# Early attention rows of a fused attention, FFN and DFT kernel: a unit's turn issued behind the next unit's scores, operands in three fixed tiles, and the second block's rows turned by TensorE

## The chip, the cores and the metric

The kernel runs on one core of a Trainium2 chip. The metric is the time of one execution on the device in microseconds (us). Five engines take part: TensorE (PE in the rows, with its weight loads as PEld), VectorE (DVE), ScalarE (ACT), GpSimd (POOL) and SyncE (SP), which here only issues transfers (DMAs). Each engine works its own instructions off in the order in which they stand, and semaphores hold it where it needs another engine's result.

## What is computed

```python
def reference(**kwargs):
    ...
    attn_out = _attn_ref(**attn_kwargs)      # 4 batches, 8 heads, 576 rows, head size 64
    x = np.ascontiguousarray(attn_out.transpose(0, 2, 1, 3)).reshape(B, S, H * D)
    x = _moe_ref(x=x, **moe_kwargs)          # LayerNorm, 512 -> 2048, relu, 2048 -> 512, + x
    return _moe2_ref(x=x, **moe2_kwargs)     # x + Re(FFT2(x)), LayerNorm, second FFN, + u
```

Attention is causal by blocks of 64 rows: a row sees the keys up to the end of its own block. The softmax is `exp(scores - max) / (sum + 1e-9)`. Weights, inputs and outputs are float32.

## The kernel before, in words

The 576 rows of a batch are cut into blocks of 256 rows: E(b), the first 256 rows of batch b, F(b), another 256, and L, the 64 rows left of each of the four batches together. The program has three long parts: the early rows E0 to E3 with the first FFN of E0 and E1 and the decoding of the first FFN's weights (the first 150 us), the attention of all other rows with the first FFN of the rest, then the DFT and the second FFN. Float32 products are made of float16 pairs (a high and a low part, three products each), and the weights, which arrive as wide words, are decoded by ACT (L214, a sign copy), DVE (L215), ACT again (a sum of squares, L236), POOL (a sum over partitions), DVE (scales), ACT (L328, the high part) and DVE (L336, the low part). The first FFN's first weight has four quarters, which the built program calls wq110 to wq113; the quarter c serves the steps mp = 2c and 2c + 1 of the FFN's first product.

**Early rows.** A batch's early rows are worked off in four units, one for each pair of heads (`e_items`, L1029). A unit loads its operands into a tile `raw` (`e_raw`, L866: a query part and two key parts, each with the other half of its partitions set to zero by POOL, L872), forms its scores on TensorE (`e_s`, L932; lines L937 and L905), takes the maximum on DVE (L951, L952) and the exponential on ACT (L955). For E0 and E1 (the tuple `ET`) the unit's exponentials are then turned, keys to partitions, by TensorE itself against a unit matrix (`e_turn`, L961; line L966), copied by ACT to a tile `PT` (L971) and multiplied with the values in float32 (`e_pv`, L983; line L990); for E2 and E3 they are split into two float16 parts (L909 on ACT, L910 on DVE) and turned by a transposing DMA (L916), and the product with the values is L885. `e_x` (L1010) divides by the sum and writes the block's rows `X`. The scores' PSUM tiles have two buffers, so a unit's scores wait until the unit before the last has left them: for E0 and E1 that is the copy L971, since the turn writes into the scores' own tile.

**LayerNorm of a block.** `ln` (L520) computes mean and scale on DVE, `ln_hi` (L554) normalizes into `xn` (L561). For E0 the normalized rows are turned by TensorE (`ln_turn`, L571: eight matmuls of line L575 into two PSUM tiles `xt`, copied by ACT at L580, the rest formed by DVE at L581). For every other block ACT and DVE make the float16 parts (`xs`, L568 and L588) and two transposing DMAs on SP's queue turn them (L589). The result `xnT` is what the block's first product waits for.

**First product.** `gemm1` (L604) is one step of 24 matmuls (L621) into one PSUM tile; ACT and DVE empty it (L630, L631). The tiles of `xt`, of `gemm1` and of the second product come from one pool (`g_tile`, L112, tag `g`), which has two buffers in this part of the program and gives them in the order in which the tiles are asked for:

```python
        ps = g_tile([128, 4, 128], "xt")      # L573, ln_turn
        ps = g_tile([128, 2, 256], "g1")      # L615, gemm1
```

**What sets the order.** `merge` (L1273) interleaves several streams of steps by weights and start times, and a scheduler then orders each engine's instructions by what is ready and by priority (`prio`). Within the streams here, `LN` holds the LayerNorm steps of E0 and E1 at a high priority, `AE` the early rows, `WA` and `WB1` the weights. `in_order` (L1265) makes a function's instructions stand behind the last TensorE instruction issued so far.

Of the kernel before, what the change touches and what calls it, by code (L numbers as in the profile page):

```python
# [8 lines left out]
F32 = mybir.dt.float32  # L9
# [11 lines left out]
NPAIR = H // 2  # L21
# [5 lines left out]
G2P = 1  # L27
ST = 2
RVE = 1
RAWE = 2  # L30
AP = 20
DW = (3, 5)
DW2 = (("G1", 1, ("F", 3), 7),) * 2 + (("F", 1, ("F", 3), 0), ("F", 1, ("F", 3), 1))
# [19 lines left out]
GSB = 2  # L53
LNQ = 200
X0B = 2
G1E = 1
LNA = 2
ESP = 20
# [38 lines left out]
def fused_kernel(ctx: ExitStack, tc: tile.TileContext, io: dict):  # L97
# [455 lines left out]

    def ln_hi(ffn, c, t):  # L554
        mv, y = lnst[ffn, c]
        own = (ffn, c) == (1, ("E", 0))
        if own:
            xn = a_tile([128, DM], F32, "xn0", "xn0")
        else:
            xn = fpool.tile([128, DM], F32, tag="xn", bufs=1, name="xn")  # L560
        nc.vector.tensor_scalar(  # L561
            out=xn, in0=X[c][:, t, :], scalar1=mv[:, t, 0:1], scalar2=y[:, t:t + 1],
            op0=ALU.subtract, op1=ALU.mult,
        )
        if own:
            return ln_turn(ffn, c, t, xn)
        xs = fpool.tile([128, 2, DM], F16, tag="xs", bufs=1, name="xs")
        nc.scalar.activation(out=xs[:, 0, :], in_=xn, func=AF.Copy)  # L568
        lnst[ffn, c, t] = (xn, xs)
# [11 lines left out]
        nc.vector.tensor_tensor(out=to[:, 1], in0=ps, in1=to[:, 0], op=ALU.subtract)  # L581

    def ln_lo(ffn, c, t):
        if (ffn, c) == (1, ("E", 0)):
            return
        xn, xs = lnst.pop((ffn, c, t))
        eng = nc.gpsimd if (ffn, t) in LNP else nc.vector
        eng.tensor_tensor(out=xs[:, 1, :], in0=xn, in1=xs[:, 0, :], op=ALU.subtract)  # L588
        nc.sync.dma_start_transpose(  # L589
            out=xnT[ffn, c].rearrange("p a k t -> p (a k) t")[:, :, t * 128:(t + 1) * 128],  # L590
            in_=xs.rearrange("p a f -> p (a f)"),
        )
# [222 lines left out]
    def a_tile(shape, dt, tag, name):  # L815
        return ap_["p"].tile(shape, dt, tag=tag, bufs=ap_["b"][tag], name=name)
# [48 lines left out]

    def e_raw(b, p):  # L866

        r = a_tile([128, 3, 256], F32, "raw", f"raw{b}{p}")
        nc.sync.dma_start(out=r[:, 0], in_=io["qt"][b, p][:, S:S + 256])
        for h in range(2):  # L870
            hs = slice(64 * h, 64 * h + 64)
            nc.gpsimd.memset(r[64 - 64 * h:128 - 64 * h, 1 + h], 0.0)  # L872
            nc.sync.dma_start(out=r[hs, 1 + h], in_=io["kt"][b, p][hs, 0:256])
        A["raw", b, p] = r

# [151 lines left out]
        )  # L1027

    def e_items(b):  # L1029
        def head():  # L1030
            e_raw(b, 0)
            e_load(b)

        def front(p):
            if p + 1 < NPAIR:
                e_raw(b, p + 1)
            e_s(b, p)
            e_exp(b, p)
            e_norm_p(b, p)

        def back(p):
            e_pv(b, p)
            e_x(b, p)

        out = [(0.0, head, (), None), (3.0, lambda: front(0), (), None)]
        if b not in ET:
            out.append((1.0, lambda: e_v(b), (), None))
        for p in range(1, NPAIR):
            out.append((3.0, lambda p=p: (front(p), back(p - EL) if p >= EL else None), (), None))
        for p in range(NPAIR - EL, NPAIR):  # L1050
            out.append((1.0, lambda p=p: back(p), (), ("X1", ("E", b)) if p == NPAIR - 1 else None))
        return out
# [455 lines left out]
    if True:  # L1508
# [28 lines left out]
            dft_setup(dctx)  # L1537

        ap_["first"] = True
        a_open(dict(stage=ST, rv=RVE, raw=RAWE, vh=2, vl=2, e=E1B[0], P=E1B[1], PT=E1B[2], xnT0=1, xn0=X0B, unit=1))  # L1540
        A["unit"] = a_tile([128, 128], F32, "unit", "unit")
        nc.gpsimd.dma_start(out=A["unit"], in_=io["c_unit"])
        w_signs(ap_["p"], WN[0], NZ[0])
        AE = [e_items(b) for b in range(B)]
# [208 lines left out]
```

## Time and profile before

| what | us |
|---|---|
| three runs, median (lowest to highest) | 994.23 (993.83 to 995.99) |
| the profiled execution | 991.83 |
| its span on the core | 990.1 |
| PE busy in the span | 925.9 (94%) |
| DVE, ACT, POOL busy in the span | 706.0, 541.5, 85.6 |
| PE waits of 0 to 60, 60 to 120 and 120 to 200 us that the profile names, summed | 14.7, 8.8, 5.8 |

The profiled execution took 1.73 us more than its span, and 2.40 us less than the median of the runs. How to read the views: a timeline's row gives the start, the length, the engine, the line and what it wrote and read, then how many instructions it merges, and in brackets how long the engine had been idle just before and what ended that. A busy PE is not PE at its peak, since matmuls are pipelined.

### The profile page before, as it was taken

The numbers are of one execution on the slowest core, as the hardware profiler recorded it, in microseconds if no ns is written. First come the engines' busy times: TensorE is split into PE (matmuls) and PEld (weight loads), VectorE is DVE, ScalarE is ACT, GpSimd is POOL, SyncE is SP. The second block draws the span as 40 slices with busy tenths as digits, with TensorE's granted clock in tenths as the row PEclk, the third lists the DMA queues.
The fourth block names the chain that finished last, engine by engine and source line by source line (L and its number), as shares of the span: only waits on it lengthen the run. The fifth ranks groups of instructions, "written<-read, shape, count | busy, mean of one in ns | idle before, by whom it ended". The sixth has DMA issues, their size and how long they took to land.

```text
span 990.1 us, 19844 instructions
## 1 busy us (share of the span) xinstructions
PE 925.9 (94%) x7794; PEld 701.4 (71%) x7794; DVE 706.0 (71%) x1753; ACT 541.5 (55%) x963; POOL 85.6 (9%) x216
## 2 busy tenths in 40 slices
PE   6797898998989898997999889999999999999998
PEld 5686744674664674856585666858588888888887
DVE  2888898777877786656597888679477675765754
ACT  4888757776776686427556544326153252342431
POOL 2101110002011020040011120100000000000000
PEclk9999999999999999999999999999999999999999
DMA  6759654677667585577318657002110101101100
GB/s 218 225 201 238 161 120 117 129 136 160 126 138 150 131 148 99 97 171 299 107 38 243 212 182 231 16 12 74 34 23 23 42 13 33 23 24 42 23 23 22
DMA packets 161566, 111.50 MB, mean 113 GB/s; under 512 B 136509, under 2 KB 143686, under 8 KB 159424
## 3 DMA queue, kind: packets, MB, share of 16 engines
q1 hardware_dynamic: 159120, 105.92, 41.9%
q0 software_dynamic: 2352, 4.32, 1.9%
q8 instruction: 61, 1.00, 0.4%
q14 instruction: 33, 0.27, 0.1%
HBM read 64.19 MB, written 11.01 MB: 76 GB/s over the span
## 4 chain that ended last, share of the span: by engine, by line
PE 47%; DVE 5%; DMA 4%; ACT 3%; issue 1%; POOL 0%; SPq 0%; ACTq 0%; POOLq 0%; DVEq 0%
PE g L692 15%; PE s L742 13%; PE g L621 9%; PE g L673 4%; PE g L646 4%; DMA wr<-in_w 3%; PE ya L1413 1%; ACT junk L236 1%; DVE ws L215 1%; DVE wq L336 1%; ACT sign L214 1%; DMA xnT2('F', 0)_8352<-xs 1%; DMA d<-ws 1%; PE pq L1447 0%; PE pv L885 0%
## 5 line engine op out<-in xcount | busy, mean ns | idle before, releaser
L621 PEld LDWEIGHTS <-wq 128*128 128x128 f16 x2112 | 206.3, 99 | 48.0 <-issue 7.8
L646 PE MATMUL g<-wq,hT 128*128 128x512 f16 x768 | 186.4, 381 | 1.3 <-ACT hT L630 1.2
L692 PEld LDWEIGHTS <-wq 128*128 128x128 f16 x1344 | 131.5, 98 | 15.4
L646 PEld LDWEIGHTS <-hT 128*128 128x128 f16 x768 | 74.1, 98 | 83.8 <-issue 2.3
L709 ACT ACTIVATE hr<-g,tk 128x256 f32<-128x256 f32 x112 | 47.0, 471 | 142.8 <-PE g L692 142.8
L742 PEld LDWEIGHTS <-hs 128*128 128x128 f16 x1176 | 115.1, 98 | 13.3
L885 PE MATMUL pv<-vh,PT 128*128 128x65 f16 (+1 forms) x704 | 97.2, 200 | 8.7 <-DMA PT<-P 4.6
L885 PEld LDWEIGHTS <-PT 128*128 128x128 f16 x1056 | 76.0, 98 | 34.2 <-issue 11.7
L717 DVE TENSOR_TENSOR hr<-hr 128x128 f32<-128x128 f32 x224 | 65.5, 292 | 48.3 <-ACT hr L709 40.4
L1134 PE MATMUL st<-k,qz 128*128 128x512 f16 (+2 forms) x288 | 80.3, 332 | 15.1 <-ACT e L1156 13.4
L1156 ACT ACTIVATE e<-st,aq,acf 128x384 f32<-128x384 f32 (+2 forms) x80 | 56.8, 741 | 52.7 <-DVE aq L1151 48.6
L910 DVE SCALAR_TENSOR_TENSOR P<-e,P 128x768 f16<-128x768 f32 (+2 forms) x56 | 54.4, 974 | 33.7 <-ACT P L909 33.4
L742 PE MATMUL s<-tT,hs 128*128 128x256 f16 x672 | 75.6, 273 | 0.0
L631 DVE SCALAR_TENSOR_TENSOR hT<-g,hT 128x512 f16<-128x512 f32 x88 | 59.8, 683 | 17.2 <-ACT hT L630 17.1
L630 ACT ACTIVATE hT<-g 128x512 f16<-128x512 f32 x88 | 51.3, 587 | 30.6 <-PE g L621 30.4
L673 PE MATMUL g<-wq,hT 128*128 128x512 f16 x288 | 64.0, 379 | 0.0
L724 DVE TENSOR_TENSOR hs<-hr,hs 128x896 f16<-128x896 f32 x56 | 60.8, 1085 | 0.5
L214 ACT ACTIVATE sign<-wr 128x512 f16<-128x512 bf16 (+1 forms) x48 | 46.4, 970 | 23.0 <-DMA wr<-in_w 22.9
L885 PE MATMUL pv<-vl,PT 128*128 128x64 f16 (+1 forms) x352 | 58.2, 199 | 0.0
L742 PE MATMUL s<-tB,hs 128*128 128x256 f16 x504 | 57.3, 273 | 0.0
L215 DVE SCALAR_TENSOR_TENSOR ws<-wr,sign 128x512 int32<-128x512 int32 (+1 forms) x48 | 41.3, 866 | 20.3 <-ACT sign L214 18.5
L723 ACT ACTIVATE hs<-hr 128x896 f16<-128x896 f32 x56 | 53.2, 949 | 1.6 <-DVE hr L717 1.6
(427 smaller groups left out, 1610.2 us busy)
## 6 DMA issues: line engine op xcount, KB each, us to landing
wr<-in_w SPq DMA_DIRECT2D x16, 1023.5 KB, 5.6
wr<-in_w SPq DMA_DIRECT2D x32, 511.8 KB, 5.1
rawv<-in_vt SPq DMA_DIRECT2D x16, 320.0 KB, 3.6
rawqk<-in_kt SPq DMA_DIRECT2D x16, 288.0 KB, 2.8
d<-ws SPq DMA_DIRECT2D x4, 1024.0 KB, 5.0
ws<-d SPq DMA_DIRECT2D x4, 1024.0 KB, 5.4
wt<-d SPq DMA_DIRECT2D x4, 1024.0 KB, 4.8
rawqk<-in_qt SPq DMA_DIRECT2D x32, 80.0 KB, 3.3
```

The costliest lines, as they stand in the source:

```text
L214: nc.scalar.activation(out=z[:, :, :, 1], in_=r.bitcast(BF16)[:, :, :, 2], func=AF.Copy)
L621: nc.tensor.matmul(out=ps[:, i, :], lhsT=w1(ffn, k, wh, m), rhs=xt[:, xh, k, :], start=(n == 0), stop=(n == 3 * KT - 1),)
L631: nc.vector.scalar_tensor_tensor(out=h[:, :, 1, :], in0=ps, scalar=0.0, in1=h[:, :, 0, :], op0=ALU.max, op1=ALU.subtract,)
L646: nc.tensor.matmul(out=ps, lhsT=h[f // 4][:, f % 4, hh, t * 128:(t + 1) * 128], rhs=w2(ffn, f, wh), start=(f == 0 and hh == 0 and wh == 0) ...
L673: nc.tensor.matmul(out=g2["b"][t], lhsT=h[f // 4][:, f % 4, hh, t * 128:(t + 1) * 128], rhs=w2(ffn, f, wh), start=(f == 0 and hh == 0 and ...
L692: nc.tensor.matmul(out=ps[:, q, :], lhsT=w1(2, k, wh, i + 8 * q), rhs=xt[:, xh, k, :], start=(n == 0), stop=(n == 3 * KT - 1),)
L717: done = nc.vector.tensor_tensor(out=r[:, o], in0=r[:, a], in1=r[:, b], op=op)
L724: nc.vector.tensor_tensor(out=h[:, 1], in0=r[:, 1:8], in1=h[:, 0], op=ALU.subtract)
L742: nc.tensor.matmul(out=ps, lhsT=h[:, hh, hb], rhs=T[nm][:, wh, i], start=(i == 0 and hh == 0 and wh == 0), stop=(i == 7 and hh == 1),)
L885: nc.tensor.matmul(out=out[..., 0:w], lhsT=l, rhs=v[..., 0:w], start=(n == 0), stop=(n == len(mm) - 1))
L1134: nc.tensor.matmul(out=st[:, h, 0:n] if j < 4 else sf[:, o:o + n], lhsT=qz[:, a, q:q + 128], rhs=k[:, c, o:o + n], start=(i == 0), stop=(j ...
L1156: nc.scalar.activation(out=e[:, h], in_=st[:, h], func=AF.Exp, scale=cf, bias=nb[:, h:h + 1],)
```

## The change

It does five things. In blocks E0 and E1 a unit's turn (`e_turn`) is issued behind the scores and exponentials of the next unit, by `in_order`, and the value product of a unit one step later still. The operands lie in three tiles `rz0` to `rz2`, made once and with their zeros written once at the start, in place of two rotating `raw` buffers whose zeros are written for every unit. Two units' loads are issued ahead of the others. A one-column exponential (`warm`) is put at the start of ACT's instructions. And the rows of E1, like those of E0, are turned by TensorE (`TURN`) and not by DMA.

```diff
-RAWE = 2
+RAWE = 3
+TURN = ((1, ("E", 0)), (1, ("E", 1)))
...
     def ln_hi(ffn, c, t):
-        own = (ffn, c) == (1, ("E", 0))
+        own = (ffn, c) in TURN
...
     def ln_lo(ffn, c, t):
-        if (ffn, c) == (1, ("E", 0)):
+        if (ffn, c) in TURN:
             return
...
     def e_raw(b, p):
-        r = a_tile([128, 3, 256], F32, "raw", f"raw{b}{p}")
+        r = A["rz"][(NPAIR * b + p) % RAWE]
         nc.sync.dma_start(out=r[:, 0], in_=io["qt"][b, p][:, S:S + 256])
         for h in range(2):
             hs = slice(64 * h, 64 * h + 64)
-            nc.gpsimd.memset(r[64 - 64 * h:128 - 64 * h, 1 + h], 0.0)
             nc.sync.dma_start(out=r[hs, 1 + h], in_=io["kt"][b, p][hs, 0:256])
...
     def e_items(b):
+        def ahead(p):
+            e_s(b, p)
+            e_exp(b, p)
+            if p > 0:
+                in_order(lambda: e_norm_p(b, p - 1))
...
-        out = [(0.0, head, (), None), (3.0, lambda: front(0), (), None)]
-        if b not in ET:
-            out.append((1.0, lambda: e_v(b), (), None))
+        if b in ET:
+            return [
+                (0.0, lambda: (e_raw(b, 0), e_raw(b, 1)), (), None),
+                (3.0, lambda: ahead(0), (), None),
+                (3.0, lambda: (e_load(b), e_raw(b, 2), ahead(1)), (), None),
+                (3.0, lambda: (e_raw(b, 3), ahead(2), back(0)), (), None),
+                (3.0, lambda: (ahead(3), back(1)), (), None),
+                (1.0, lambda: (e_norm_p(b, 3), back(2)), (), None),
+                (1.0, lambda: back(3), (), ("X1", ("E", b))),
+            ]
+
+        out = [(0.0, head, (), None), (3.0, lambda: front(0), (), None), (1.0, lambda: e_v(b), (), None)]
...
-        a_open(dict(stage=ST, rv=RVE, raw=RAWE, vh=2, vl=2, e=E1B[0], P=E1B[1], PT=E1B[2], xnT0=1, xn0=X0B, unit=1))
+        a_open(dict(stage=ST, rv=RVE, rz=RAWE, warm=1, vh=2, vl=2, e=E1B[0], P=E1B[1], PT=E1B[2], xnT0=1, xn0=X0B, unit=1))
+        warm = a_tile([128, 1], F32, "warm", "warm")
+        nc.vector.memset(warm, 0.0)
+        nc.scalar.activation(out=warm, in_=warm, func=AF.Exp)
         A["unit"] = a_tile([128, 128], F32, "unit", "unit")
+        A["rz"] = [a_tile([128, 3, 256], F32, "rz", f"rz{i}") for i in range(RAWE)]
+        for z in A["rz"]:
+            for h in range(2):
+                nc.gpsimd.memset(z[64 - 64 * h:128 - 64 * h, 1 + h], 0.0)
```

The built order of the changed program, at three places. First PE at the start of the program (`st_122` holds the scores of E0's first unit, `st_151` those of its second, `st_180` those of its third; line numbers are those of the changed kernel):

```order
L937 MATMUL st_122<-rz0_104 128x256 x2
...
L937 MATMUL st_151<-rz1_105 128x128 x2
...
L937 MATMUL st_151<-rz1_105 128x256 x2
...
L966 MATMUL st_122<-unit_103,e_131 128x128 x6
L990 MATMUL pv_206<-rv0_142,PT_175 128x65 x6
L937 MATMUL st_180<-rz2_106 128x128 x2
```

Before, the first unit's turn stood between the scores of the first and the second unit, and the first value product behind the scores of the third; now the turn stands behind the second unit's scores, and the value product ahead of the third's.

Second, ACT around the copies of E0's turned rows (`xt_307`, `xt_316`). `e_405` or `e_422` is the exponential of E1's second unit, `wq111` the sum of squares of the second quarter and `sign20` the decoding of a weight piece. Before:

```order
L955 ACTIVATE e_422<-st_413,eq_423 128x128 x2
L955 ACTIVATE e_422<-st_413,eq_423 128x256 x2
L580 ACTIVATE xnT0_304<-xt_307 128x4x128
L580 ACTIVATE xnT0_304<-xt_316 128x4x128
L214 ACTIVATE sign20_102<-wr1120_383 128x1024
```

Now:

```order
L955 ACTIVATE e_405<-st_396,eq_406 128x128 x2
L955 ACTIVATE e_405<-st_396,eq_406 128x256 x2
L237 ACTIVATE wq111_426,wn_368<-ws111_365 128x2048
L215 ACTIVATE sign20_114<-wr1120_363 128x1024
L581 ACTIVATE xnT0_304<-xt_307 128x4x128
L581 ACTIVATE xnT0_304<-xt_316 128x4x128
```

The sum of squares stood two instructions ahead of that exponential and now stands behind it; the decoding of the next piece stood behind the copies and now stands ahead of them.

Third, PE around the turn of E1's rows (`xt_701`, `xt_710`) in the changed program. `st_1060` and `st_1145` are the scores of E2's third and fourth unit, `g1_749` is step mp = 4 of E0's first product:

```order
L576 MATMUL xt_701<-unit_103,xn0_699 128x128
L576 MATMUL xt_710<-unit_103,xn0_708 128x128
...
L937 MATMUL st_1060<-rz1_105 128x256 x2
...
L937 MATMUL st_1145<-rz2_106 128x128 x2
...
L937 MATMUL st_1145<-rz2_106 128x256
L622 LDWEIGHTS wq112_590
L622 MATMUL g1_749<-xnT0_304,wq112_590 128x256
```

Before, E0's steps mp = 4 and 5 stood right behind mp = 3, and mp = 6 and 7 among the scores of E2's units, with no turn of E1's rows on PE; now the steps mp = 4 to 7, 96 matmuls, stand behind the turn and behind nearly all scores of E2.

## Rows read from the trace of the kernel before

**Rows 1.** The page: the span, and the engines' busy time in it.
```profile
span 990.1 us, 19844 instructions
PE 925.9 (94%) x7794; PEld 701.4 (71%) x7794; DVE 706.0 (71%) x1753; ACT 541.5 (55%) x963; POOL 85.6 (9%) x216
```

**Rows 2.** By stretch: length, busy PE, PEld, DVE, ACT, POOL, granted clock, DMA.
```profile
66.00:88.00 22.00, 16.13 (x137) 13.38 (x134) 20.21 (x58) 18.12 (x27) 3.46 (x9) 0.99 0.72 211
88.00:124.00 36.00, 32.21 (x337) 27.20 (x338) 29.88 (x85) 30.02 (x53) 3.28 (x10) 0.96 0.74 190
124.00:150.00 26.00, 23.40 (x155) 11.38 (x153) 22.89 (x52) 15.63 (x28) 4.50 (x10) 1.00 0.52 114
```

**Rows 3.** What PE waited for, 60 to 155 us: total, times, longest.
```profile
PE g L621 <- DMA xnT1('E', 1)_683<-xs: 5.1, 1, 5.1
PE pv L885 <- DMA PT<-P: 4.6, 4, 1.5
PE st L1134 <- ACT qz L1116: 1.6, 1, 1.6
```

**Rows 4.** Timeline of the first 12 us, PE and ACT.
```profile
4.25 1.41 PE L937 MATMUL st<-raw 128*128 128x128 f32 x4 [4.25 <-POOL raw L872]
...
9.08 1.28 ACT L955 ACT_TABLE_LOAD   x1 [9.08 <-DVE eq L952]
10.38 1.36 ACT L955 ACTIVATE e<-st,eq 128x128 f32<-128x128 f32 x4
```

**Rows 5.** Timeline of 34 to 46 us: E0's LayerNorm to its first product.
```profile
34.73 0.68 DVE L526 BATCH_NORM_STATS2 bn1('E', 0)0_286<-XxE 128x6 f32<-128x512 f32 x1
...
41.40 2.06 PE L575 MATMUL xt<-unit,xn 128*128 128x128 f32 x16 [2.15 <-DVE xn L561]
...
43.28 1.08 ACT L580 ACTIVATE xnT<-xt 128x512 f16<-128x512 f32 x2 [0.17 <-PE xt L575]
...
45.93 1.15 PE L621 MATMUL g<-xnT,wq 128*128 128x256 f16 x9
```

**Rows 6.** ACT by line, 44 to 88 us: busy us, mean ns, idle before.
```profile
L214 ACT ACTIVATE sign<-wr 128x1024 f16<-128x1024 bf16 x8 | 10.9, 1360 | 0.0
L328 ACT ACTIVATE wq<-ws,gs 128x512 f16<-128x512 f32 x12 | 7.8, 726 | 0.8 <-DVE gs L323 0.8
L236 ACT ACTIVATE wq<-ws 128x2048 bf16<-128x2048 f32 x4 | 7.6, 1910 | 2.4 <-DVE pw L841 2.2 <-DVE ws L215 0.2
...
L955 ACT ACTIVATE e<-st,eq 128x128 f32<-128x128 f32 (+1 forms) x12 | 4.1, 430 | 0.9 <-DVE eq L952 0.9
```

**Rows 7.** Timeline of 64 to 93 us: E0's steps, E2's scores, E1's turn.
```profile
64.87 6.82 PE L621 MATMUL g<-xnT,wq 128*128 128x256 f16 x61
...
77.02 0.54 DVE L561 TENSOR_SCALAR xn<-XxE,ln1('E', 1)_664 128x512 f32<-128x512 f32 x1
...
80.00 0.39 PE L937 MATMUL st<-raw 128*128 128x128 f32 x2
...
81.29 0.69 PE L937 MATMUL st<-raw 128*128 128x128 f32 x4
...
82.90 1.34 ACT L214 ACTIVATE sign<-wr 128x1024 f16<-128x1024 bf16 x1
...
84.00 1.25 SPq L589 DMA_TRANSPOSE xnT1('E', 1)_683<-xs  x1
...
88.17 4.24 PE L621 MATMUL g<-xnT1('E', 1)_683,wq 128*128 128x256 f16 x24 [5.13 <-DMA xnT1('E', 1)_683<-xs]
```

**Rows 8.** Timeline of PE, 100 to 151 us.
```profile
100.88 2.67 PE L621 MATMUL g<-xnT1('E', 1)_683,wq 128*128 128x256 f16 x23
...
121.58 1.91 PE L621 MATMUL g<-xnT1('E', 1)_683,wq 128*128 128x256 f16 x16
...
139.82 0.20 PE L885 MATMUL pv<-vh,PT 128*128 128x65 f16 x1 [0.98 <-DMA PT<-P]
...
150.13 0.32 PE L1134 MATMUL st<-k,qz 128*128 128x384 f16 x1 [1.61 <-ACT qz L1116]
```

## The prediction, made blind

> **What bounds the kernel now.** I read the page first, for the shares. PE is busy for 925.9 of 990.1 us [rows 1], so there is little to gain outside of its waits, and those of the first 200 us, which alone the change touches, are the ones to price. The order of every engine's instructions is the same before and after from the point where the attention of the other rows begins; its first scores start at 150.13 [rows 8]. A shift of that start is carried one to one to the end, so everything below is worked out up to there. Then the windows: from 66 to 88 us DVE is busy for 20.21 of 22.00, ACT for 18.12, and PE for only 16.13, and from 88 to 124 both are still at 30 of 36 [rows 2]. In that part the decoding of the weights sets the pace and PE waits for it; from about 90 us PE is full again. Then PE's waits by releaser: 5.1 in one wait for E1's rows turned by DMA, 4.6 in four waits for PT, the exponentials turned by DMA, and 1.6 for the attention's first query operand [rows 3].
>
> **Up to 46 us: about 0.** The table load of 1.28 at 9.08 stands ahead of the first exponential at 10.38 [rows 4]; a one-column exponential moves it to ACT's idle start, so the first unit's exponentials come up to 1.3 earlier. The second unit's scores no longer wait for the first turn. But the value product of unit 0 now stands ahead of the third unit's scores and waits for ACT's copy, which takes part of this back. By walking the new orders with the old durations I get the statistics of E0's LayerNorm at 33.6 in place of 34.73 [rows 5]. On the way from there to the first product, ACT now decodes a weight piece (a mean of 1.36 [rows 6]) ahead of the copies which began at 43.28, and DVE has some 2 us of decoding and maxima ahead of its half. So the copies start at 43.1 and the first product at 46.0, against 45.93 [rows 5]. Bounds: -1.1, if the earlier statistics go through, and +1.2, if they are lost and the piece is in the way. The zeros that POOL no longer writes are off the path, POOL being at 9% [rows 1].
>
> **46 to 66 us: a gain that ends nowhere.** Nearly all scores of E1's last two units now lie ahead of the first product; 0.69 for four records of 128 columns and what follows to the next unit make a unit's scores about 1.3 (80.00 to 81.29 [rows 7]). So mp = 3, which was done at 64.87 + 13 x 0.11 = 66.3 (61 matmuls in 6.82 [rows 7], 13 of them its own), is done at about 64. These 2 us are hidden: what stands next waits for another engine.
>
> **E1's turn on PE: +5.2.** Before, E1's rows went through two DMAs; the second was issued at 84.00 and the product began at 88.17, after 5.13 of idle [rows 7]. This idle goes. But in the new order E0's mp = 4 to 7, which filled PE from 73.93 on, stand behind the turn, and they ask for the two buffers of tag g which the turned rows hold. They cannot start until ACT's and DVE's copies have emptied them. So PE idles earlier instead, and the 96 matmuls come out of the cover.
>
> When do the copies run? On ACT, between E0's copies (43.28 + 1.08, less 0.3 of pipelining) and E1's copies, the new order has 7 sign copies, 3 sums of squares, 12 high parts, 16 pieces of exponentials, 3 PT copies, 4 copies of mp = 0 to 3, one value part and one P. By the groups [rows 6], each taken at its distance to the next instruction (group busy over count: 1.36 less 0.12 of overlap, 1.90, 0.61 and about 0.31) this is 7 x 1.24 + 3 x 1.90 + 12 x 0.61 + 16 x 0.31 = 26.7, and 5.9 for the others, together 32.6 us. From 44.1 that ends at 76.7 with no idle. ACT had 22.00 - 18.12 = 3.9 of idle in the 22 us before 88 [rows 2]; I take 2.5, since the scores are earlier now, but DVE, whose results ACT waits for, is at 92%. So the copies start at 79.3. The other gate agrees: E1's `xn` was at 77.02 [rows 7], and 16 records of the turn took 2.06 for E0 [rows 5]. With E0's measure from copy to first product (43.28 to 45.93, 2.65 [rows 5], of which DVE's half is the end; I take 2.0, as the first buffer suffices for mp = 4) this step starts at 81.3. Four steps of 24 matmuls at 2.62 are 10.5: 91.8. The clock adds to that. After its 5.13 of idle 24 matmuls took 4.24 [rows 7], warm 23 of them 2.67 [rows 8], and the granted clock of 88 to 124 is 0.96, where 66 to 88 has 0.99 [rows 2]; 4.24 - 2.7 gives 1.5, and I put 1.6 behind the longer gap (bounds 0 and 1.6). E1's product begins at 93.4 against 88.17: +5.2.
>
> The Trainium skill, page "Perfetto Trace Analysis", section "Matmuls", asks that independent groups of matmuls rotate through different PSUM banks, so that emptying one overlaps the next. By that mp = 4 would run right behind the turn, at about 77.7, and the sum would be 3.6 lower; the built order gives it the very buffers that E1's rows hold.
>
> **Back to 150 us.** E1's own product no longer begins cold: -1.5 (the 4.24 above, already counted ahead of it). Three quarters of the scores of E2's last unit, formerly behind its start, are done: -1.0 (from the same 1.3). Of the four waits for PT [rows 3] the first three, 4.6 - 0.98 = 3.6, I get at 4.2, because exponentials of E2 and E3 come to stand behind copies of mp = 2 and 4: +0.6. So E1's first product, which ended at 121.58 + 16 x 0.11 = 123.3 [rows 8], is done 3.3 later. Then there is slack: the last wait for PT, 0.98 at 139.82 [rows 8], is for work of ACT and DVE that is not shifted with PE, so it goes: -1.0. And the 1.61 at 150.13 [rows 8] is the end of a chain that starts with that product and takes 10.3 us; in the new order the product stands some ten wide matmuls earlier, about 2 us, and the chain is covered: -1.6.
>
> **Sum:** 0 + 0 + 5.2 - 1.5 - 1.0 + 0.6 - 1.0 - 1.6 = +0.7. The profiled execution of 991.83 (span 990.1 and 1.73 outside) becomes 992.5; it lies 2.40 under the median of the runs, so the time forecast for the median is 994.23 + 0.7 = **994.9**. A difference of 0.2%, about 2 us, is what a measurement of this kernel can tell from no change, and this is inside of it.
>
> **The rivals.** *Faster.* ACT waits for nothing on the way to E1's copies, mp = 4 starts at 78.8 (2.5 less), and with everything earlier the waits for PT shrink to 1.5 of 4.2 (2.7 less): 0.7 - 5.2 = -4.5, so 989.7. It decides if mp = 4 starts before about 79. For it speaks that E1's rows leave the DMA's way, where the last part was issued at 84.00 and took 4.17 to the product [rows 7], while a turn on PE is 2.06 [rows 5]. The Trainium skill, page "VectorE: DVE Perf Modes", sections "The three transpose paths" and "Rules for kernel authors", gives TensorE 390 ns and a DMA 1309 ns for a 128 x 128 turn of bf16 and prefers TensorE if the result may lie in PSUM; the trace agrees in direction. Against it speaks DVE at 92% in that stretch [rows 2] and the held buffers.
>
> *Slower.* The wait moves instead of going: ACT idles on the way to E1's copies at the rate of before, 3.9 in 22 [rows 2], which over 32.6 of work is 5.8 and not 2.5, +3.3. mp = 4 is held to 84.6, PE's idle ahead of it grows by as much, and all 96 matmuls follow: +4.0, 998.2, with lost PT cover up to +7. It decides if mp = 4 starts after about 83. For it speaks that ACT's idle before was for DVE, the sums of squares having 2.4 of idle in front and the high parts 0.8 [rows 6], and the change makes DVE no shorter but for the two `xs` steps.
>
> *It doesn't do what it says.* The built order shows the turns moved, E1's matmuls on PE and its transposing DMAs gone; no chance.
>
> **How the numbers follow.** The forecast has 0.38: its sum has terms of 5 and its result is under 1, so small errors move it out of the 2 us. Slower has 0.35, as the mechanism of the held buffers is plain and its size is not; faster 0.27. The range goes from the faster rival's 989.7, rounded to 989.5, to 999.5, the slower rival's 998.2 with part of its PT cover lost. The forecast's own range is 993.0 to 996.2.
>
> **What would show it.** In the profile of the changed kernel: E0's first product near 46; mp = 3 done near 64; the first matmul of mp = 4, behind E1's turn and an idle stretch that ends with the copies or with ACT, near 81; E1's product near 93 with no wait ahead of it and 24 matmuls in 2.7; three waits for PT of some 4 us; the attention's first scores near 151 without a wait for the query operand. If mp = 4 is at 79 or 84 a rival has it. If the start of the attention moves and the end doesn't follow by the same, the premise that later parts carry the shift is wrong.

## The result, and the profile after

The changed kernel takes 1002.56 us (median of 5 runs, 1000.39 to 1006.73) against 993.83 for the kernel before (5 runs, 992.53 to 995.99): a ratio of 1.0088, 95% interval 1.0065 to 1.011. It is slower by 8.7 us, on the slower rival's side and past the end of the range. The profiled execution took 1002.56 as well, with a span of 1000.7.

The page of the changed kernel, span and busy time (against [rows 1]): PE is busy 5.0 us longer for nearly the same work.

```profile
span 1000.7 us, 19779 instructions
PE 930.9 (93%) x7810; PEld 708.1 (71%) x7810; DVE 705.4 (70%) x1754; ACT 541.3 (54%) x964; POOL 77.1 (8%) x190
```

What PE waited for in the changed kernel, first from 0 to 60 us, then from 60 to 120 (total, times, longest; against [rows 3]):

```profile
PE st L966 <- ACT e L955: 4.4, 2, 2.9
PE st L937 <- DMA rz<-in_kt: 4.1, 1, 4.1
PE pv L990 <- issue: 3.0, 1, 3.0
PE st L937 <- ACT PT L971: 1.8, 2, 0.9
...
PE st L937 <- ACT e L955: 7.3, 1, 7.3
PE pv L885 <- DMA PT<-P: 2.9, 1, 2.9
PE g L622 <- DVE hT L632: 2.6, 3, 1.2
```

Up to 60 us the waits sum to 13.3, less than the 14.7 of the kernel before. And yet E0's first product is 6.5 us late. The timeline of PE in the changed kernel shows where:

```profile
14.93 1.52 PE L990 MATMUL pv<-rv,PT 128*128 128x65 f32 x12 [3.05 <-issue]
...
29.30 2.13 PE L966 MATMUL st<-unit,e 128*128 128x128 f32 x12 [1.48 <-ACT e L955]
...
39.86 2.43 PE L966 MATMUL st<-unit,e 128*128 128x128 f32 x12 [2.88 <-ACT e L955]
...
44.33 2.06 PE L937 MATMUL st<-rz 128*128 128x256 f32 x4
...
46.25 2.51 PE L576 MATMUL xt<-unit,xn 128*128 128x128 f32 x16
...
52.41 0.27 PE L622 MATMUL g<-xnT,wq 128*128 128x256 f16 x1
...
72.10 1.11 PE L937 MATMUL st<-rz 128*128 128x256 f32 x4
...
80.58 0.80 PE L937 MATMUL st<-rz 128*128 128x128 f32 x2 [7.31 <-ACT e L955]
81.36 3.70 PE L576 MATMUL xt<-unit,xn 128*128 128x128 f32 x16
...
87.28 10.80 PE L622 MATMUL g<-xnT,wq 128*128 128x256 f16 x96
98.76 1.47 PE L622 MATMUL g<-xnT1('E', 1)_698,wq 128*128 128x256 f16 x12 [0.67 <-DVE hT L632]
...
158.26 0.32 PE L1149 MATMUL st<-k,qz 128*128 128x384 f16 x1 [0.38 <-ACT qz L1131]
```

The same four score matmuls take 2.06 at 44.33 and 1.11 at 72.10. The windows of the changed kernel say why; the column behind POOL is the granted clock (columns as in [rows 2]):

```profile
16.50:20.00 3.50, 3.50 (x16) 2.89 (x16) 1.43 (x5) 0.00 (x0) 0.00 (x0) 0.51 1.02 419
...
30.20:33.60 3.40, 3.40 (x18) 3.16 (x16) 2.57 (x3) 2.99 (x6) 0.00 (x0) 0.50 0.30 123
...
40.40:47.30 6.90, 6.00 (x26) 5.10 (x25) 3.66 (x15) 4.97 (x8) 0.39 (x1) 0.51 0.92 331
47.30:78.00 30.70, 25.96 (x230) 24.07 (x229) 26.41 (x73) 27.53 (x44) 0.96 (x2) 1.00 0.60 199
78.00:84.80 6.80, 4.22 (x18) 3.94 (x19) 6.22 (x22) 6.80 (x12) 0.77 (x2) 0.50 0.43 154
```

In four stretches PE ran at 1.2 GHz and not at 2.4, three shortly behind a wait (3.05 at 14.93, 1.48 at 29.30, 2.88 at 39.86), the fourth from within one (7.31, up to 80.58). Three of them lie ahead of E0's first product. The trace of the kernel before has none from 20 to 50 us:

```profile
20.00:30.00 10.00, 8.93 (x76) 8.39 (x76) 6.78 (x23) 8.86 (x15) 1.00 (x3) 1.00 0.94 314
30.00:40.00 10.00, 6.12 (x47) 5.05 (x45) 9.29 (x27) 6.30 (x11) 1.36 (x5) 1.00 0.67 194
40.00:50.00 10.00, 8.60 (x77) 8.07 (x78) 8.29 (x23) 9.78 (x16) 1.12 (x3) 1.00 0.66 228
```

PE was busy for 3.5 + 3.4 + 6.0 + 4.2 = 17.1 us of the four slow stretches; at the full clock the same work is half, 8.6 us less. That is as large as the loss, but it is a bound and no proof. Part of it could have been hidden in later waits, and the kernel before has slow work too: E1's first 24 matmuls took 4.24 there [rows 7], some 1.5 more than warm ones, and at its start E0's first turn took 2.93 for matmuls that took 1.60 in E1's first, although the clock column reads 1.00 at both:

```profile
11.79 2.93 PE L966 MATMUL st<-unit,e 128*128 128x128 f32 x12 [4.05 <-ACT e L955]
...
37.64 1.60 PE L966 MATMUL st<-unit,e 128*128 128x128 f32 x12 [2.88 <-ACT e L955]
```

The trace of the kernel before is also that of a short execution: 991.83, where the shortest of all its timed runs is 992.53. Two kernels of the experiments below, e1_turn_alone and before_fill, have its order of instructions on every engine up to E0's first product. They start that product at 48.7 and 46.6 and not at 45.9, and in each the clock fell within the same wait of 2.88, so that E1's first turn took 2.93 (half speed from 36.9 to 47.1 us in the first, from 37.9 to 41.3 in the second):

```profile
37.76 2.93 PE L966 MATMUL st<-unit,e 128*128 128x128 f32 x12 [2.88 <-ACT e L955]
...
38.31 2.93 PE L969 MATMUL st<-unit,e 128*128 128x128 f32 x12 [2.88 <-ACT e L958]
```

The changed kernel's order up to there is found in three traces (the change, undo_e1_turn, after_own_psum). All three have the three early stretches and start the product at 52.4 to 52.6. So the new order is 3.7 to 6.7 us late, and part of the 6.5 is luck of the one trace of the kernel before. What the clock costs, the experiments had to tell.

The first of the waits is made on ACT. In the changed kernel ACT copies E0's first turned unit behind the next unit's exponentials and behind the decoding of a weight piece:

```profile
11.59 1.36 ACT L955 ACTIVATE e<-st,eq 128x128 f32<-128x128 f32 x4 [1.36 <-DVE eq L952]
12.82 1.36 ACT L215 ACTIVATE sign<-wr 128x1024 f16<-128x1024 bf16 x1
14.02 0.81 ACT L971 ACTIVATE PT<-st 128x768 f32<-128x768 f32 x1
```

### The profile page after: what moved, and what is told of

It reads as the page before. It is cut to its first block, busy times and chain, and to the rows that moved or that the text cites. A ratio compares the mean times of both kernels' runs of the same rounds, so it can differ in the third digit from the quotient of the medians.

```text
span 1000.7 us, 19779 instructions
## 1 busy us (share of the span) xinstructions
PE 930.9 (93%) x7810; PEld 708.1 (71%) x7810; DVE 705.4 (70%) x1754; ACT 541.3 (54%) x964; POOL 77.1 (8%) x190
## 4 chain that ended last, share of the span: by engine, by line
PE 44%; DVE 6%; DMA 5%; ACT 3%; issue 1%; POOL 0%; SPq 0%; ACTq 0%; POOLq 0%; DVEq 0%
PE g L693 15%; PE s L743 13%; PE g L622 7%; PE g L674 4%; DMA wr<-in_w 4%; PE g L647 3%; DVE wq L337 1%; ACT junk L237 1%; DVE ws L216 1%; ACT sign L215 1%; PE ya L1428 1%; DMA xnT2('F', 0)_8322<-xs 1%; DVE hT L632 1%; DMA d<-ws 1%; PE pq L1462 0%
## 5 line engine op out<-in xcount | busy, mean ns | idle before, releaser
L743 PEld LDWEIGHTS <-hs 128*128 128x128 f16 x1176 | 115.1, 98 | 13.3
L885 PEld LDWEIGHTS <-PT 128*128 128x128 f16 x1056 | 76.0, 98 | 33.6 <-issue 10.6
L215 ACT ACTIVATE sign<-wr 128x512 f16<-128x512 bf16 (+1 forms) x48 | 46.5, 969 | 20.6 <-DMA wr<-in_w 20.1
L216 DVE SCALAR_TENSOR_TENSOR ws<-wr,sign 128x512 int32<-128x512 int32 (+1 forms) x48 | 41.3, 865 | 20.5 <-ACT sign L215 18.4
```

Of the source, the lines that this page charges most:

```text
L215: nc.scalar.activation(out=z[:, :, :, 1], in_=r.bitcast(BF16)[:, :, :, 2], func=AF.Copy)
L743: nc.tensor.matmul(out=ps, lhsT=h[:, hh, hb], rhs=T[nm][:, wh, i], start=(i == 0 and hh == 0 and wh == 0), stop=(i == 7 and hh == 1),)
L885: nc.tensor.matmul(out=out[..., 0:w], lhsT=l, rhs=v[..., 0:w], start=(n == 0), stop=(n == len(mm) - 1))
```

## The experiments

Each ratio is to the kernel before on the same chip, with its 95% interval. "First" and "E1's" are the starts of E0's and E1's first product in the one profiled execution. "Slow" is 2 x (1 - mean granted clock) x time, the mean over the timed runs: how long PE's clock stood at 1.2 GHz by that column (the slow rows at the very start of an execution are not in it). The kernel before has 27 to 30 us of it in these comparisons. A trace is one execution, a ratio compares medians of 4 to 25 runs; a kernel and its variant were not always timed on the same chip.

| kernel | ratio | interval | first | E1's | slow |
|---|---|---|---|---|---|
| the change | 1.0088 | 1.0065 to 1.011 | 52.4 | 98.8 | 37 |
| undo_e1_turn | 1.0052 | 1.003 to 1.0073 | 52.4 | 90.7 | 40 |
| e1_turn_alone | 1.0074 | 1.0049 to 1.01 | 48.7 | 104.5 | 32 |
| undo_order | 1.0136 | 1.0104 to 1.0169 | 50.8 | 103.3 | 37 |
| order_alone | 1.0021 | 0.9997 to 1.0045 | 45.3 | 83.7 | 36 |
| no_rz | 1.0038 | 1.0014 to 1.0061 | 44.7 | 92.7 | 29 |
| before_fill | 0.9973 | 0.9951 to 0.9995 | 46.6 | 89.2 | 20 |
| order_alone_fill | 0.9905 | 0.9878 to 0.9933 | 46.2 | 84.3 | 20 |
| after_fill | 0.9957 | 0.9933 to 0.998 | 49.7 | 96.1 | 23 |
| after_own_psum | 0.9969 | 0.9947 to 0.999 | 52.6 | 87.4 | 29 |
| after_own_psum_fill | 0.9858 | 0.9819 to 0.9896 | 45.5 | 80.5 | 12 |
| no_rz_own_psum | 0.9927 | 0.9906 to 0.9948 | 44.8 | 82.4 | 22 |
| best_dma_fill | 0.9956 | 0.9934 to 0.9978 | 46.5 | 95.9 | 27 |
| after_dve_copy | 1.0047 | 1.0012 to 1.0081 | 49.1 | 95.6 | 40 |
| no_rz_own_psum_fill | 0.9923 | 0.9892 to 0.9954 | 47.1 | 82.2 | 19 |
| undo_e1_turn_fill | 0.9904 | 0.9874 to 0.9934 | 46.3 | 85.6 | 13 |

### Which part of the change costs

The first theory was the prediction's own large term: E1's turned rows hold the buffers of `mp` = 4 to 7. Its rival: the new order of the units costs, up to the first product.

undo_e1_turn, the change without E1's turn:

```diff
-TURN = ((1, ("E", 0)), (1, ("E", 1)))
+TURN = ((1, ("E", 0)),)
```

> The changed kernel with E1's rows turned by DMA again (TURN holds E0 alone). If the loss is made by the new order of E0's and E1's units (first product at 52.4 in place of 45.9), this keeps it: first product near 52, time 997 to 1000. If it is made by E1's turn and the two PSUM buffers that it holds against mp = 4 to 7, it goes: 993 to 996, even with the first product late.

Measured 1.0052 (1001.42 us, a little above the first case), first product at 52.4: more than half of the loss stays. e1_turn_alone, the kernel before with that part only:

```diff
-        own = (ffn, c) == (1, ("E", 0))
+        own = (ffn, c) in ((1, ("E", 0)), (1, ("E", 1)))
...
-        if (ffn, c) == (1, ("E", 0)):
+        if (ffn, c) in ((1, ("E", 0)), (1, ("E", 1))):
             return
```

> The kernel before with E1's rows turned by TensorE and nothing else. In the built order mp = 3 to 7 then stand behind the turn. If the loss is made by the order of the units: first product near 46 and 993 to 997. If by the turn and its buffers: PE waits some 8 us ahead of mp = 3 or the turn, 999 to 1003.

Measured 1.0074 (1003.42 us): this costs too, by itself nearly as much as the whole change. The clock has a part in it: the trace is at half speed from 36.9 to 47.1 us (its turn is shown above) and from 74.4 to 84.7. Its waits between 60 and 110 us, on PE:

```profile
PE xt L575 <- DVE xn L561: 3.9, 1, 3.9
PE st L937 <- ACT e L955: 2.9, 1, 2.9
PE st L937 <- DMA raw<-in_kt: 2.2, 1, 2.2
```

undo_order puts the units' old steps back into the changed kernel (in `e_items` the block `if b in ET: return [...]` goes, and the line that it replaced returns).

> The changed kernel with the units' old order (a unit's turn right behind its own scores), with the three fixed tiles, the one-column exponential and E1's turn by TensorE kept. If the loss is made by the order: first product near 45 and 992 to 996. If by E1's turn: 999 to 1003. Against the kernel with E1's turn alone it shows what the three tiles and the early table load are worth; I expect -1 to 0.

Measured 1.0136 (1009.63 us), the worst of all, with a first product at 50.8, where both theories had 1003 at most. PE waits 8.3 us for E1's `xn` there; why DVE makes it so late was not followed up. Against e1_turn_alone the three tiles and the early table load were to be worth -1 to 0; the kernel is 6.2 us slower. order_alone adds the new steps to the kernel before:

```diff
+        def ahead(p):
...
+        if b in ET:
+            return [
...
```

> The kernel before with the units' new order alone (two rotating operand tiles, zeros written for every unit, no one-column exponential, E1's rows by DMA). If the loss is made by the order: first product near 52, granted clock at half speed in stretches between 16 and 50 us, 998 to 1002. If by E1's turn: 993 to 996.

Measured 1.0021, not told from 1. The rival falls with it: the first product is at 45.3, and of the gain of 4.5 us at E1's product (83.7 against 88.17) 0.9 is left when attention starts (149.2 against 150.1). The profiled execution is 8.1 us longer than that of the kernel before all the same; its loss lies behind that start, at a mean granted clock of 0.982 against 0.991 over the whole, and is not explained. So the parts don't add: order, fixed tiles and E1's turn each cost in some company and not in other. What these five kernels share is the last column, 32 us and more at half speed. In order_alone the windows show two such stretches where the early gain disappears:

```profile
81.90:88.70 6.80, 5.02 (x24) 3.59 (x25) 5.13 (x14) 6.26 (x12) 0.38 (x1) 0.50 1.06 217
95.50:98.90 3.40, 3.40 (x18) 2.64 (x16) 1.33 (x2) 2.31 (x3) 0.00 (x0) 0.51 0.95 319
```

### The clock

Second theory: PE's waits in the early part let its clock fall, and the work behind them at half speed is the loss. To test it, matmuls of the unit matrix are issued where PE idles, into a PSUM tile that the next product overwrites. In two pairs of kernels, the change and after_fill, after_own_psum and after_own_psum_fill, the traces show all other instructions of every engine in the same order with the filling as without. In the other pairs with and without a filling the order behind it changed as well, so they show what a kernel gained and not what the clock alone does.

no_rz first, which was still on the order: rotating operand tiles, three of them, in the changed kernel.

```diff
-        r = A["rz"][(NPAIR * b + p) % RAWE]
+        r = a_tile([128, 3, 256], F32, "raw", f"raw{b}{p}")
...
+            nc.gpsimd.memset(r[64 - 64 * h:128 - 64 * h, 1 + h], 0.0)
```

> The changed kernel with rotating operand tiles again (three of them, zeros written for every unit); order, one-column exponential and E1's turn are kept. In the built order the third unit's scores then stand ahead of the first value product, and ACT's first copy of PT behind one exponential piece and not four. If the fixed tiles (through the order that they lead to) cost the first 50 us: E0's first product at 44 to 47 in place of 52.4, and 997 to 1000. If the new order of the units costs it by itself: 51 to 53 and 1001 to 1004.

Measured 1.0038, first product at 44.7, as the first case had it, with a time of 1000.62, just above its 1000. The order that the fixed tiles lead to does have the late first product. With no more time at half speed than the kernel before (29 us against 28) no_rz is still slower; its E1's product is at 92.7, 48.0 behind the first.

before_fill and order_alone_fill have the same edit, in `gemm1`:

```diff
         ps = g_tile([128, 2, 256], "g1")
+        if (ffn, c, mp) == (1, ("E", 1), 0):
+            for _ in range(18):
+                nc.tensor.matmul(out=ps[:, 0, 0:128], lhsT=A["unit"], rhs=A["unit"], start=True, stop=True)
```

> The kernel before with 18 matmuls of the unit matrix put into the PSUM tile of E1's first product ahead of it, where PE idles for 5.13 us; they are overwritten and change nothing else in the order. If the granted clock falls because PE idles, it stays at full speed from 87 to 91 us, E1's first 24 matmuls take 2.7 and not 4.24, and the time is 1 to 2 lower, 992 to 995. If the clock falls for another reason, the row stays at 4.2 and the time within 1.

Measured 0.9973 (993.17 us, in the first case). E1's first 24 matmuls took 2.78, against 4.24 [rows 7]. Against the expectation, the order behind E1's product changed with the filling.

> The new order alone, with the same 18 matmuls ahead of E1's first product. That kernel had E1's product 4.5 us earlier than the kernel before, and lost all of it behind it, with the clock at half speed from 81.9 to 88.7 and from 95.5 to 99.0. If the clock took the gain: full speed from 80 to 100, attention 3 to 4 us earlier, 992 to 996. If waits for PT did: attention within 1 of 149 and 997 to 999.

Measured 0.9905 (987.65 us, below the first case): with the added 4.18 us of matmuls that kernel is 1.2% faster than without. Attention starts 3.0 us earlier (146.2 against 149.2), as the first case had it. The larger part of the gain lies behind that, where the trace of order_alone was slow; and the order behind E1's product is another here. On the timeline of order_alone E1's first 24 matmuls took 5.24:

```profile
83.68 5.24 PE L621 MATMUL g<-xnT1('E', 1)_710,wq 128*128 128x256 f16 x24 [4.14 <-DMA xnT1('E', 1)_710<-xs]
```

on that of order_alone_fill 2.78, at nearly the same start:

```profile
79.20 4.18 PE L618 MATMUL g<-unit 128*128 128x128 f32 x36
...
84.33 2.78 PE L624 MATMUL g<-xnT1('E', 1)_710,wq 128*128 128x256 f16 x24
```

after_fill puts ten matmuls ahead of E0's first turn and ten ahead of E1's first, in the tile of the value product that follows:

```diff
+    def fill(b, p, n):
+        ps = pso.tile([128, 2, 2, 65], F32, tag="o", name="pv")
+        for _ in range(n):
+            nc.tensor.matmul(out=ps[:, 0, 0], lhsT=A["unit"], rhs=A["unit"][:, 0:65], start=True, stop=True)
+        A["pvt", b, p] = ps
```

> The changed kernel with 10 matmuls of the unit matrix ahead of E0's first turn and 10 ahead of E1's first, into the PSUM tile of the value product that follows (overwritten); all else stands in the same order. PE idles 3.05 and 2.88 us there. If the clock makes the early loss: fewer than 7 us at half speed between 16 and 48 (17.1 in the changed kernel), first product at 48 to 50 in place of 52.4, time 2 to 4 lower, 998 to 1001. If the waits make it: first product at 52 to 54 and no less time.

Measured 0.9957 (992.87 us, well below the first case): from slower than the kernel before to faster, by twenty matmuls whose result nobody reads, with every other instruction in the same order. The clock still fell once ahead of the first product in the profiled execution (27.4 to 34.2), and the first product is at 49.7; both are as the first case had them. (Its 17.1 for the changed kernel is the busy time in all four slow stretches; the three up to 48 us are 13.8 long.) The profiled execution, the second longest of ten, shows only part of the gain: attention starts 2.0 us earlier than in the changed kernel (156.3 against 158.3). Nor does the last column carry all of it: 14 us less at half speed are 7 us of work, and the ratios differ by 13 us.

### The buffers

Third theory: with the clock aside, the held buffers still cost. after_own_psum takes them out:

```diff
-        ps = g_tile([128, 4, 128], "xt")
+        ps = g_tile([128, 4, 128], "xt") if c == ("E", 0) else pso.tile([128, 4, 128], F32, tag="o", name="xt")
```

> The changed kernel with the PSUM tiles of E1's turned rows taken from the value products' pool and not from the two buffers of tag g. In the built order mp = 4 to 7 then stand ahead of the turn again. If the held buffers make E1's product late (46.4 us behind E0's first product in the changed kernel, 42.3 in the kernel before): 38 to 41 behind it, PE's wait of 7.3 at 80 us gone, ratio to the kernel before 1.001 to 1.005 (1.0088 in the changed kernel). If ACT and DVE set it anyway: 45 or more behind and 1.007 to 1.010.

Measured 0.9969, better than the first case. The first product is still at 52.6, but E1's follows 34.8 behind it and not 46.4. Most of that lead is lost again by the start of attention, 155.2 against 158.3, with half speed from 112.5 to 115.9 and from 126.1 to 129.5 us, where the changed kernel has none. Its timeline has the turn in the middle of `mp` = 6 and 7, and no wait of 7.3:

```profile
80.56 2.06 PE L576 MATMUL xt<-unit,xn 128*128 128x128 f32 x16
82.46 3.22 PE L622 MATMUL g<-xnT,wq 128*128 128x256 f16 x28
...
87.37 3.77 PE L622 MATMUL g<-xnT1('E', 1)_698,wq 128*128 128x256 f16 x33
```

after_own_psum_fill has both edits.

> The same with the 2 x 10 matmuls of the unit matrix ahead of E0's and E1's first turns. If the early clock and the held buffers are two separate costs, their gains add: 0.987 to 0.993. If they are the same time seen twice, it is no better than the better of the two alone (0.9957 with the matmuls).

Measured 0.9858, 981.98 us against 996.44, just past the first case: the two are separate costs, and their gains add (0.0131 and 0.0119 alone, 0.0230 together). This and after_own_psum are the clearest pair: the same order on the same chip, 981.98 us and 994.12. In the traces the first product is 7.1 earlier than without the filling, E1's 6.9, attention 10.1 (145.1 against 155.2) and the end 12.2, with 3.5 us at half speed ahead of attention and not 20.4. Timeline of PE, with the two fillings (L964):

```profile
8.97 2.42 PE L964 MATMUL pv<-unit 128*128 128x65 f32 x20
...
32.74 2.42 PE L964 MATMUL pv<-unit 128*128 128x65 f32 x20
35.79 1.60 PE L974 MATMUL st<-unit,e 128*128 128x128 f32 x12 [0.62 <-ACT e L955]
...
45.55 0.27 PE L622 MATMUL g<-xnT,wq 128*128 128x256 f16 x1
```

and its windows: full clock from 7.5 up to 99 us.

```profile
7.50:50.00 42.50, 37.38 (x308) 34.39 (x308) 27.91 (x82) 31.28 (x55) 1.29 (x4) 1.00 0.85 264
50.00:99.00 49.00, 45.37 (x425) 39.81 (x423) 45.97 (x120) 46.41 (x74) 3.21 (x6) 1.00 0.77 220
```

This is the fastest kernel of the study. no_rz_own_psum joins the edits of no_rz and after_own_psum, with no filling.

> Rotating operand tiles (three), the new order, the one-column exponential, and E1's turn in PSUM tiles of its own: the change without its two costs and with no added matmul. If the fixed tiles' order and the held buffers are all of the loss: 0.990 to 0.996. If E1's turn on TensorE costs by itself: 0.998 to 1.004.

Measured 0.9927, within the first case. best_dma_fill is order_alone_fill with three rotating tiles and the one-column exponential:

```diff
-RAWE = 2
+RAWE = 3
...
+        nc.scalar.activation(out=warm, in_=warm, func=AF.Exp)
```

> The new order, three rotating operand tiles, the one-column exponential, E1's rows by DMA, and 18 matmuls of the unit matrix ahead of E1's product. Against the same with two tiles and without the exponential (0.9905): if the third tile and the early table load help, 0.985 to 0.989; if not, 0.989 to 0.993.

Measured 0.9956, a miss, outside of both cases: another order came out, in which a value product of E2 stands ahead of E1's product and waits for its DMA. Its row on PE:

```profile
92.47 0.20 PE L888 MATMUL pv<-vh,PT 128*128 128x65 f16 x1 [4.05 <-DMA PT<-P]
```

### What was left open

after_dve_copy shortens the first wait and adds no matmul:

```diff
+        if (b, p) == (0, 0):
+            nc.vector.tensor_copy(out=et, in_=st[:, :, 0:384])
+        else:
+            nc.scalar.activation(out=et, in_=st[:, :, 0:384], func=AF.Copy)
```

> The changed kernel with the copy of E0's first turned unit on VectorE, which idles there, and not on ACT, where it stands behind four exponential pieces and a sign copy. PE's wait ahead of the first value product falls from 3.05 to about 1. If idle time lowers the clock: no half-speed stretch at 16.5, first product 1 to 4 earlier than 52.4, ratio 1.003 to 1.007. If it does not: the stretch stays, first product 1 to 2 earlier, ratio as before (1.0088).

Measured 1.0047, first product at 49.1: between the two kernels, as the clock theory has it, with an interval (1.0012 to 1.0081) that overlaps the changed kernel's (1.0065 to 1.011). Over its timed runs it was no less at half speed (40 us against 37), so it is the trace that speaks for the theory here, and not the ratio. The wait ahead of the first value product is 1.17 there (3.05 in the changed kernel), and the windows are at full clock up to 26.8; the later stretches stay, since their waits do:

```profile
9.80:26.80 17.00, 13.28 (x107) 12.09 (x107) 9.92 (x27) 11.27 (x21) 0.39 (x1) 1.00 0.99 300
26.90:30.30 3.40, 3.40 (x17) 3.16 (x17) 2.62 (x3) 3.00 (x6) 0.00 (x0) 0.50 0.39 153
37.10:43.90 6.80, 5.90 (x26) 5.00 (x25) 3.62 (x15) 4.92 (x8) 0.38 (x1) 0.50 0.94 333
```

no_rz_own_psum_fill and undo_e1_turn_fill combine edits shown above.

> Rotating operand tiles, new order, own PSUM for E1's turn and the 2 x 10 matmuls ahead of the first turns. If the fixed tiles cost only through the clock: within 0.003 of 0.9858, the same with fixed tiles. If their order costs by itself: 0.975 to 0.982.

Measured 0.9923: neither case. It is the same as without the filling (0.9927) and no better than with fixed tiles (0.9858), so no cost of the fixed tiles shows here. But it is no clean test: the order differs from that without the filling from 39 us on, and the clock was held less well than with fixed tiles (19 us at half speed against 12). What the fixed tiles' order costs by itself stays open.

> The changed kernel with E1's rows by DMA, the 2 x 10 matmuls ahead of the first turns and 18 ahead of E1's product: the clock is held in all three places. If E1's turn on TensorE (in PSUM of its own) is a gain: 0.989 to 0.994, against 0.9858 with it. If it is worth nothing: 0.984 to 0.988.

Measured 0.9904, in the first case. Against 0.9858 that speaks for a gain by E1's turn in PSUM of its own, but the intervals (0.9874 to 0.9934, 0.9819 to 0.9896) overlap; it stays open.

## Why the prediction was wrong

| start of | before | predicted | changed kernel | after_own_psum_fill |
|---|---|---|---|---|
| E0's first product | 45.9 | 46.0 | 52.4 | 45.5 |
| `mp` = 4 | | 81.3 | 87.3 | |
| E1's product | 88.2 | 93.4 | 98.8 | 80.5 |
| attention | 150.1 | 151 | 158.3 | 145.1 |

**The step that failed is "Up to 46 us: about 0".** It walked the new order with durations of the old rows, which are at full clock from 20 us on; the upper bound of +1.2 had no clock in it. The clock was priced at one place only, behind the gap at E1's turn. In the changed kernel it fell three times before that, and the first product came 6.5 late. With the clock held, after_own_psum_fill has the first product at 45.5 in an order that up to there differs from the changed kernel only by the fillings. after_own_psum, the same without them, has it at 52.6. (Some of these 7.1 us is the difference between two executions: the first value product is already 1.3 apart.) So the walk through the order was near, though with luck: its old durations up to 16 us are slow ones, and after_own_psum_fill had fast ones from 7.5 us on. Of the 7.4 us by which attention started later than the sum has it, 6.4 lie in this step and 2.1 behind E1's product; E1's turn gave 1.1 back.

**46 to 66 us.** `mp` = 3 was done at 67.82 + 2.35 = 70.2, 17.8 behind the first product, where 18 was forecast.

**E1's turn, +5.2: the cause and the place were right; 4.1 came.** `mp` = 4 was to start 35.3 us behind the first product by the working, and started 34.9 behind it. The idle stretch was to lie between the turn and `mp` = 4. It lies ahead of the turn: scores of E2 that stand there wait 7.31 for an exponential on ACT, and the 96 matmuls that could fill the time stand behind the turn, because its tiles have their buffers. No row shows `mp` = 4 itself waiting for a buffer. E1's product was forecast 47.4 behind the first and came 46.4 behind. Where the working put 1.6 for a cold clock behind the gap, the clock was paid in the turn: in the changed kernel the 96 matmuls took 10.80, which is the full clock, and the fall from 78.0 to 84.8 hit the turn, 3.70 against 2.06 [rows 5], and scores. The working of ACT's share came out too: from E0's copies to E1's it was busy 33.24 of 35.30 us (49.70 to 85.00), where 32.6 and 2.5 of idle time were put down. after_own_psum shows the buffers as the cause: with tiles of another pool the 96 matmuls stand ahead of the turn, and the wait is gone. The Trainium skill, page "Perfetto Trace Analysis", section "Matmuls", which asks for different PSUM banks for independent groups, was the rule to weigh more: it was said to be worth 3.6 us here, and the ratio went from 1.0088 to 0.9969.

**Back to 150 us, -4.5: half of it came.** From E1's product to the start of attention the delay shrank from 10.6 to 8.1. E1's product with what stands among it was to take 1.9 less than before and took as long: it began warm, but three waits for DVE's half of `hT` (2.6, the first of them, 0.67, ahead of E1's product) are new. Of the 2.6 behind it 2.2 came, by other shares than worked out: the wait for the query operand fell from 1.61 [rows 8] to 0.38, and the last one for PT, 0.98 before [rows 8], stayed at 0.86.

**The tail.** From attention on the delay was to be carried one to one, the order being the same from there on: 8.1 there, 8.7 between the medians, 10.7 between the two profiled executions. It was not quite so. The two orders are the same only from about 180 us of the kernel before, and up to there the scores wait longer for exponentials (1.8 us from the start of attention on in the kernel before, 3.9 in the changed one). The same scores, first before and then now:

```profile
167.06 0.38 PE L1134 MATMUL st<-k,qz 128*128 128x512 f16 x1 [0.65 <-ACT e L1156]
...
178.67 0.38 PE L1149 MATMUL st<-k,qz 128*128 128x512 f16 x1 [1.72 <-ACT e L1171]
```

So the delay is 11.6 there. Behind 180 us, with the same order in both, it goes up and down between 8.2 and 12.5 and ends at 10.6. From the start of attention to the end the traces of all kernels here take 836 to 849 us, so single executions differ by more than that.

**The rivals.** The slower one had the direction and one of the two mechanisms, the held buffers, but not its own deciding point: ACT's idle time on the way to E1's copies was 2.1 and not 5.8; everything only came later. `mp` = 4 was "after 83" because the first product was late. The faster one's gain (4.5 us) came only in kernels from which both costs were removed, and there more came (after_own_psum_fill, 0.9858).

The two causes are shown by taking them out, one at a time and together: filling the early waits gives time back with no other instruction moved, the PSUM tiles give time back by the order that they allow, and the two gains add. Not shown is what decides whether a given wait lowers the clock. The wait ahead of E1's first turn is 2.88 in the kernel before, e1_turn_alone, before_fill and the changed kernel; the first kept the clock there and the others lost it. And the gains by ratio are larger than the work that the slow stretches cost, so part of their size stays unexplained.

## What to carry to other kernels

Before an order is walked with old durations, mark each wait of TensorE that it makes or moves, and price the work behind it at half speed as well: here that price, 8.6 us, was as large as the loss. Where a short wait can't be taken out, a handful of matmuls into a PSUM tile that is overwritten anyway can be worth over 1% (1.0088 to 0.9957, 0.9969 to 0.9858), or nothing (0.9927 to 0.9923); look whether the order changed with them. A tile that is turned in PSUM holds a buffer until two engines have emptied it, so look who is next in the same pool.

## What the runs showed of the hardware

The clock fell behind waits as short as 1.48 us (at 29.30, with others before it); the four stretches at half speed in the changed kernel are 3.4 to 6.9 us long. Executions of the same order differ: up to E0's first product the kernel before kept the clock from 20 us on, before_fill was at half speed for 3.4 us and e1_turn_alone for 10.2. The time goes with it: the changed kernel's five runs go from 1000.39 at a mean granted clock of 0.985 to 1006.73 at 0.974. The Trainium skill, page "TensorE: Matmul & The Clock Gate", section "HAM oscillation — how this bites in real kernels", describes a wait that lets TensorE be throttled so that the next tile starts cold; the trace agrees, with 2.06 against 1.11 us for the same four matmuls. The waits in that example of the Trainium skill are DMA waits of 3 to 5 us; here waits for ACT of 1.48 to 3.05 went before the falls. The Trainium skill, page "Perfetto Trace Analysis", section "Matmul Optimizations", says that matmuls should run back to back, since the engine scales its power with its use; no run here shows power, but the advice held even for matmuls of no use, 1.0088 to 0.9957.
